# Steps 150 to 687 of a hand-written step list in a new order, in a fused clustered-attention and SiLU kernel

## The chip, the cores and the metric

The kernel runs on one core of a Trainium2 chip. The metric is device time in microseconds (us) of one execution; 302.02 us is the median of three runs of the kernel before (301.93 to 302.09).

## The reference

Attention over 4 batches and 8 heads, 768 tokens of 64 values each, in which a query attends only to keys whose nearest centroid (of 16 per head) is its own; its result, 3072 tokens of 512 values, goes through two matrix products with a SiLU between them.

```python
q_assign = np.argmax(np.einsum('bhsd,hcd->bhsc', q_n, c_n), axis=-1)
k_assign = np.argmax(np.einsum('bhsd,hcd->bhsc', k_n, c_n), axis=-1)
mask = q_assign[:, :, :, None] == k_assign[:, :, None, :]
scores = np.where(mask, scale * np.matmul(q, k.transpose(0, 1, 3, 2)), -1e9)
attn = softmax(scores)                      # over the keys
x = np.matmul(attn, v)                      # heads side by side: 3072 x 512
h = x @ w_in                                # 512 -> 2048
out = (h * sigmoid(h)) @ w_out              # 2048 -> 512
```

## The kernel before

**The order of the work is a list.** All the work after the first loads is issued by one list of 1559 words, `plan`, in the kernel's last function. Each word is a step: a name, a number, and behind a point either an engine (A is ACT, D is DVE, P is POOL) or the numbers of the PSUM banks that it opens. The function `step` turns a word into instructions. The kernel runs in a manual schedule, so the instructions of an engine, and the DMAs of a queue, are issued in the order of the list; semaphores keep only what depends on one another apart. An engine whose next instruction isn't ready waits with all that stands behind it. SP (the queue that issues most DMAs) and POOL (which issues some) are such queues too.

**Loading a head.** Job n is one head of one batch (32 in all; jobs 0 to 7 and two extra ones, `x`, carry batch 0). `r` loads its q and k in float32 (L92). `hi` scales them and rounds to float16 (L103 on ACT, L105 on POOL, L107 on DVE), `lo` takes the remainder (L112, DVE). `ht` transposes both by a DMA from SP into the tile `ab` (L121); in batch 0 `tr`, `xp` and `xq` do this on TensorE (PE) and `ev`, `xu`, `xw` copy it out of PSUM. `vl` loads v (L264, from SP or, with P, from POOL) and `v` rounds it (L270 on ACT, L272 on DVE or POOL).

**Assigning clusters.** `L`, `xL` and `l` multiply by the centroids (PE, L159), `ls`, `mx` and `ge` sum, find the maximum and compare (DVE, L168, L183, L192), `cm` transposes the marks (PE, L221), `ce` copies them out of PSUM (L232 on ACT, L234 on DVE) and sends them by a DMA from SP (L235) into rows of `ab`, where they act as the mask. From job 16 on `cs`, `cx` and `cv` do this by DMAs.

**Attention.** `qk` N (PE, L325, two products of 384 columns) writes scores into one of two PSUM buffers apart from the banks; `ex` N (ACT, L330) takes their exponential P. So `qk` N waits for `ex` N-2. There are 192 of them: 24 for each of 4 batches and 2 halves of the queries. `pa` to `py` and `pv` multiply P by v (PE, L342, 36 small products for two heads), `nm` normalizes (DVE, L352 and L354), and `pt` with `pe` (PE L363, then L372 on ACT or L374 on DVE), or `xd` (a DMA), transposes the result into `xt`.

**The SiLU part.** For each half of a batch there are 16 blocks: `e` (PE, L390, four products; `a` issues three of them ahead), `t` (ACT, tanh, L402), `g` (DVE, L405). The second matrix product is done for pairs of 128-token tiles with seven products instead of eight: `m` (PE, L477, eight matmuls each) on sums of tiles (`S`, DVE, L490) and on sums of weights (`wc`, DVE, L443), `z` and `o` write out. `w` loads the weights by DMAs from POOL (L526, L529), each behind a tiny copy (L522) that waits for the last `ex` listed ahead of it.

**Banks.** Four PSUM banks (0 to 3) are passed from step to step. A step that opens a bank waits for the step that read the earlier contents out: `e` for the `g` before it there, `pv` for a `nm`, `L` for a `ce`, `pt` for a `pe`, as the list says.

Of the kernel before, what the change touches and what calls it, by code (L numbers as in the profile page):

```python
# [29 lines left out]
def kernel(  # L30
# [573 lines left out]
    def step(op, n, eng, banks):  # L604
# [124 lines left out]
        w3 L7.1 w7 qk11 ex10 ex11 xL0.0 xM0 mx7 ge7 cm7 pb0 qk12 xm0 xg0 xh1.D ce7.A v2 xc0 pc0 xe0.D ex12 qk13 pa1.0  # L729
        qk14 pc1 nm0 pt0.3 w2 ex13 qk15 xl1 w5 v6.D pb1 hi8.D nm1 ex14 qk16 ex15 qk17 ex16 ex17 hi10.P w10 xq1.1 xp1.2  # L730
        xu1.D qk18 qk19 pa2.0 pb2 w6 w4 od0 v12.D xw1.D ex18 qk20 pt1.2 hi9.D pe1.D pc2 nm2 ex19 qk21 xL1.2 ex20 w8
        xM1 ex21 qk22 qk23 pt2.0 ex22 ex23 xm1 px3.1 qk24 pe0.D lo8 xg1 xc1 py3 qk25 ex24 qk26 pe2.D a1.0 xe1.A nm3
        pt3.1 pe3.D a0.2 ex25 ex26 qk27 ex27 e1 e4.1 e0 t4 g4 vl10 qk28 t0 g0 qk29 ex28 e6.3 t6 g6 ex29 vl11.P e3.1 t3
        w9 e2.2 t2 ht8 qk30 ex30 t1 qk31 g3 r12 lo9 w11 r13 e13.1 t13 g1 g13 qk32 pv4.3 g2 nm4 ex31 qk33 ex32 ex33
        vl14 e5.1 t5 qk34 ex34 lo10 g5 ht10 qk35 e11.3 qk36 ex35 qk37 pv5.0 nm5 ex36 t11 g11 pt4.2 qk38 wc0 ex37 e14.1
        qk39 ex38 ex39 hi11.D e8.0 ht9 lo11 pe4.A t14 t8 qk40 e12.2 ex40 ht11 g14 L8.3 qk41 qk42 t12 g12 ex41 ex42 g8
        mx8 ge8 e7.1 v11 qk43 e9.0 wc4 cm8 ce8.D v10 t7 g7 wc8 ex43 qk44 e10.1 qk45 t9 g9 wc1 hi13.A lo13 t10 S3 wc5
        wc2 e15.2 ex44 ex45 pt5.0 pe5.A wc9 qk46 L10.3 r14 ht13 r15 g10 hi12.A mx10 ex46 lo12 ht12 r17 qk47 ex47 ge10
        pv6.0 nm6 pv7.1 t15 g15 pt6.0 cm10 ce10.A l9.2 pe6.A wc6 nm7 pt7.1 pe7.A ls9 wc3 mx9 ge9 qk48 L11.2 ex48
        hi14.A e20.1 t20 l13.0 cm9.3 ce9.A mx11 ge11 wc12 cm11 ls13 qk49 qk50 ex49 g20 lo14 ht14 S1 e23.0 t23 ce11.A  # L740
        g23 e27.3 t27 g27 wc13 e18.1 t18 e16.2 wc7 hi15.A l12.0 ls12 e22.3 g18 ex50 t16 vl8 r18 wc10 g16 hi17.A lo15
        vl9 ht15 e21.0 t21 e25.1 t25 g21 g25 qk51 ex51 e30.2 t30 qk52 mx12 ge12 g30 r16 ex52 e29.0 t29 g29 e26.1 qk53
        qk54 t26 g26 t22 g22 lo17 ht17 e19.2 ex53 e24.1 cm12.0 L14.3 t19 g19 mx14 ge14 ex54 qk55 qk56 ce12.A t24 g24
        mx13 ge13 hi18.D r19 e31.2 ex55 ex56 l15.0 cm14 ce14.A ls15 e28.1 t28 g28 qk57 ex57 qk58 hi16.D e17.3 cm13.0
        m1.1 qk59 m7 lo16 wc14 S2 mx15 v8 ce13.A t31 ex58 t17 vl13 g17 ht16 od2 v9 pv8.0 nm8 qk60 g31 S13 ge15 ex59
        pv9.3 wc11 lo18 qk61 ex60 qk62 z0 m6 wc15 ex61 S4 qk63 cm15.0 vl15 ex62 ex63 m2.2 ht18 ce15.D z1 qk64 ex64 S11
        nm9 xd9 qk65 m5 v15 hi19.A ex65 v13 m11.0 m17 v14.D S12 qk66 z2 o3 lo19 ht19 ex66 l17.3 ls17 qk67 ex67 m3 qk68
        l16.3 r20 r23 xd8 mx17 ls16 o0 m4 qk69 ex68 z10 vl17 qk70 ex69 o1 ex70 pv10.2 od1 m16 ge17 cs17 z11 l18.3 qk71
        qk72 nm10 mx16 o2 xd10 r21 ex71 ex72 S23 ls18 m15 z12 o13 pv11.2 qk73 ex73 hi20.D ge16 nm11 m12.1 l19.3 m14
        S14 o12 ls19 lo20 o10 qk74 ex74 qk75 ex75 pt11.2 m13 pe11.A qk76 m21.3 mx18 mx19 r22 qk77 o11 e36.1 ex76 e34.0  # L750
        ex77 ht20 t36 z20 t34 qk78 ex78 m22.2 qk79 S21 S22 m26 cs16 ge18 ex79 hi21.D g34 o20 hi23.D lo21 pv12.2 vl18
        nm12 qk80 ht21 e35.0 qk81 z21 hi22.P ex80 t35 lo23 ex81 m25 z22 cx16 ht23 qk82 ex82 v18.D e37.2 m27 g36 o23
# [77 lines left out]
```

## Time and profile before

| what | value |
|---|---|
| time, median of 3 runs | 302.02 us |
| time of the profiled execution | 301.82 us |
| its span, first to last instruction | 300.0 us |
| granted TensorE clock | 0.999 |
| PE busy | 289.6 us, 97% |
| ACT busy | 235.3 us, 78% |
| DVE busy | 222.3 us, 74% |
| POOL busy | 67.1 us, 22% |
| DMA traffic | 44.13 MB, 147 GB/s over the span |

Around the span lie 1.82 us. Busy shares are means over a program whose stages differ, so they are read by stretches of time, given in us from the start of the span. A matmul of 384 columns is counted as busy for about 0.33 us, while in a row one follows the other after 0.16 us, so a PE that counts as busy can still be waiting a little. Steps 150 to 687 run from about 27 to 130 us.

### The profile page before, as it was taken

The numbers are of one execution on the slowest core, as the hardware profiler recorded it, in microseconds if no ns is written. First come the engines' busy times: TensorE is split into PE (matmuls) and PEld (weight loads), VectorE is DVE, ScalarE is ACT, GpSimd is POOL, SyncE is SP. The second block draws the span as 40 slices with busy tenths as digits, with TensorE's granted clock in tenths as the row PEclk, the third lists the DMA queues.
The fourth block names the chain that finished last, engine by engine and source line by source line (L and its number), as shares of the span: only waits on it lengthen the run. The fifth ranks groups of instructions, "written<-read, shape, count | busy, mean of one in ns | idle before, by whom it ended". The sixth has DMA issues, their size and how long they took to land.

```text
span 300.0 us, 8619 instructions
## 1 busy us (share of the span) xinstructions
PE 289.6 (97%) x3457; PEld 215.3 (72%) x3457; DVE 222.3 (74%) x488; ACT 235.3 (78%) x413; POOL 67.1 (22%) x121
## 2 busy tenths in 40 slices
PE   7899899889999999999999999999999999999995
PEld 3767666566688877767876787766866887777684
DVE  5898646899999597768758995788766734667673
ACT  5998899988988767898888975898759768974621
POOL 2656803000202004042664312111320000000000
PEclk9999999999999999999999999999999999999999
DMA  6999999999996899785569758479122102211103
GB/s 209 285 259 248 176 205 247 206 210 176 213 178 134 173 237 186 212 200 111 124 155 191 206 107 143 147 162 179 37 70 67 28 1 72 73 39 36 37 20 123
DMA packets 75688, 44.13 MB, mean 147 GB/s; under 512 B 54288, under 2 KB 71728, under 8 KB 75648
## 3 DMA queue, kind: packets, MB, share of 16 engines
q1 hardware_dynamic: 71136, 36.93, 53.8%
q0 software_dynamic: 4224, 6.36, 11.7%
q8 instruction: 27, 0.44, 0.6%
q10 hardware_dynamic: 288, 0.30, 0.3%
q14 instruction: 13, 0.11, 0.1%
HBM read 27.30 MB, written 6.29 MB: 112 GB/s over the span
## 4 chain that ended last, share of the span: by engine, by line
PE 79%; DMA 7%; DVE 5%; ACT 5%; issue 2%; POOL 1%; SPq 0%; ACTq 0%; POOLq 0%
PE ph L390 24%; PE xb L477 20%; PE pS L325 17%; PE pO L342 9%; DMA vn<-in_v_dram 5%; PE yb L477 3%; PE psN L159 3%; ACT P L330 2%; DMA raw<-in_q_dram 1%; DMA ab<-cd 1%; PE wb L477 1%; DVE hl L112 1%; DVE gt L405 1%; ACT hl L103 1%; ACT ab L144 1%
## 5 line engine op out<-in xcount | busy, mean ns | idle before, releaser
L330 ACT ACTIVATE P<-pS 128x768 f16<-128x768 f32 x192 | 151.2, 816 | 25.3 <-PE pS L325 24.7
L390 PE MATMUL ph<-xt,win_s 128*128 128x384 f16 x512 | 96.8, 326 | 1.6 <-DVE gt L405 1.0
L405 DVE SCALAR_TENSOR_TENSOR gt<-tn,ph 128x384 f16<-128x384 f32 x128 | 68.0, 550 | 27.8 <-ACT tn L402 26.9
L325 PE MATMUL pS<-ab 128*128 128x384 f16 x384 | 87.2, 326 | 1.1 <-DMA ab<-cd 0.6
L390 PEld LDWEIGHTS <-win_s 128*128 128x128 f16 x512 | 49.4, 98 | 33.4 <-issue 2.5
L402 ACT ACTIVATE tn<-ph 128x384 f32<-128x384 f32 x128 | 61.6, 500 | 12.5 <-PE ph L390 9.6
L325 PEld LDWEIGHTS <-ab 128*128 128x128 f16 x384 | 34.2, 97 | 16.4 <-issue 1.9
L342 PEld LDWEIGHTS <-P 128*128 128x128 f16 x1152 | 39.8, 97 | 4.1 <-ACT P L330 0.5
L477 PEld LDWEIGHTS <-gt 128*128 128x128 f16 x384 | 37.1, 98 | 7.2
L342 PE MATMUL pO<-vt,P 128*128 128x65 f16 x1152 | 41.2, 193 | 0.4 <-ACT P L330 0.4
L112 DVE SCALAR_TENSOR_TENSOR hl<-raw,hl 128x768 f16<-128x768 f32 (+3 forms) x35 | 31.9, 913 | 0.7 <-ACT hl L103 0.5
L477 PEld LDWEIGHTS <-s 128*128 128x128 f16 x288 | 27.9, 98 | 5.1
L272 POOL CAST vt<-vn 128x384 f16<-128x384 f32 x19 | 12.4, 661 | 55.1 <-DMA vn<-in_v_dram 55.1
L477 PE MATMUL xb<-wout_s,gt 128*128 128x256 f16 x192 | 24.6, 273 | 0.0
L499 ACT ACTIVATE ot<-xb 128x256 f32<-128x256 f32 x36 | 13.8, 384 | 11.5 <-PE xb L477 11.1
L477 PE MATMUL xb<-wc,s 128*128 128x256 f16 x176 | 22.8, 273 | 0.0
L159 PEld LDWEIGHTS <-ab 128*128 128x128 f16 x544 | 19.2, 97 | 4.3 <-issue 0.8
L199 POOL TENSOR_SCALAR od<-od 128x96 f16<-128x96 f16 x16 | 8.4, 525 | 55.0 <-DVE od L192 54.9
L159 PE MATMUL psN<-stk,ab 128*128 128x16 f16 (+1 forms) x544 | 20.0, 184 | 0.6 <-DVE xt L374 0.6
L105 POOL TENSOR_SCALAR hl<-raw 128x768 f16<-128x768 f32 (+1 forms) x8 | 16.3, 2034 | 12.9 <-ACT P L330 7.0
L354 DVE TENSOR_TENSOR xn<-pO,zr 128x384 f16<-128x384 f32 x32 | 17.8, 558 | 1.1
L508 DVE SCALAR_TENSOR_TENSOR ot<-xb,ot 128x256 f32<-128x256 f32 x20 | 8.5, 423 | 13.8 <-ACT ot L499 5.5
(90 smaller groups left out, 257.5 us busy)
## 6 DMA issues: line engine op xcount, KB each, us to landing
raw<-in_k_dram SPq DMA_DIRECT2D x31, 192.0 KB, 4.0
vn<-in_v_dram SPq DMA_DIRECT2D x25, 192.0 KB, 4.1
raw<-in_q_dram SPq DMA_DIRECT2D x24, 192.0 KB, 3.3
out_dram<-ot SPq DMA_DIRECT2D x18, 256.0 KB, 3.0
win_s<-in_moe_w_in_dram POOLq DMA_DIRECT2D x8, 256.0 KB, 7.1
wout_s<-in_moe_w_out_dram POOLq DMA_DIRECT2D x4, 512.0 KB, 9.6
out_dram<-ot SPq DMA_DIRECT2D x12, 128.0 KB, 1.7
vn<-in_v_dram POOLq DMA_DIRECT2D x7, 192.0 KB, 3.1
```

What stands on the lines that cost most here:

```text
L105: nc.gpsimd.tensor_scalar(out=o, in0=i, scalar1=QS, scalar2=None, op0=ALU.mult)
L112: nc.vector.scalar_tensor_tensor(out=hl[:, s, 1, :], in0=raws[job.name][:, s, :], scalar=QS, in1=hl[:, s, 0, :], op0=ALU.mult, op1=ALU.sub ...
L159: nc.tensor.matmul(L[:, n % 2, :, n // 2], ab[:, i, :], stk[:, job.groups[i // 3][0], x : x + w], start=(x == 0), stop=(x + w == 2 * HC),)
L325: nc.tensor.matmul(pS[:, e, 0:HALF], abs_[kj.name][:, kn, :], rhs, start=True, stop=True)
L330: nc.scalar.activation(out=P, in_=pst.pop(u)[:, :, 0:HALF], func=AF.Exp, bias=0.0, scale=ESC)
L342: nc.tensor.matmul(o[:, (2 * t + h) * VW : (2 * t + h + 1) * VW], Ps[i + h, c, j // 2][:, j % 2, ts(t, 128)], vtb[(i + h) % 13][:, j, 0:VW ...
L354: nc.vector.tensor_tensor(out=xn, in0=ov[:, :, 0:D], in1=zr.unsqueeze(2).to_broadcast([128, 2 * NM, D]), op=ALU.mult)
L390: nc.tensor.matmul(ph[:, 0:HALF], win_s[:, r, ts(fb, 128)], xts[b, c][:, r, :], start=(r == 0), stop=(r == NR - 1))
L402: nc.scalar.activation(out=tn, in_=phs[b, c, fb][:, 0:HALF], func=AF.Tanh, bias=0.0, scale=0.5)
L405: nc.vector.scalar_tensor_tensor(out=gt[:, fb, NM * c : NM * c + NM, :].rearrange("p t n -> p (t n)"), in0=tns.pop((b, c, fb)), scalar=1.0 ...
L477: nc.tensor.matmul(o, self.lhs(l, f), self.rhs(r, f), start=(f == 0 and opens), stop=(f == HB - 1), skip_group_check=True)
L499: nc.scalar.activation(out=o, in_=self.xb[:, 0:DH], func=AF.Copy, bias=0.0, scale=0.5)
```

## The change

The list is the only thing that differs. It has the same 1559 steps before and after; the first 150 and all from step 688 on are word for word the same. In between, steps stand in another order, and 75 have another engine or bank. Nothing is added or removed in the computation. One line of each, out of the 66 that differ:

```diff
-        xM1 ex21 qk22 qk23 pt2.0 ex22 ex23 xm1 px3.1 qk24 pe0.D lo8 xg1 xc1 py3 qk25 ex24 qk26 pe2.D a1.0 xe1.A nm3
+        pt0.3 xp1.0 xu1.D qk18 qk19 pa2.0 pc2 w10 vl11.P nm1 ex18 qk20 pb2 nm2 ex19 qk21 ex20 ex21 qk22 ex22 xL1.1
```

Steps that change engine: from ACT to DVE `xe1`, `pe4`, `pe5`, `pe7`, `hi17`, `ce14`, `pe11`; from DVE to ACT `pe1`, `ce8`, `hi16`, `hi20`, `v18`; from DVE to POOL `hi9`, `hi11`, `hi23`, `v17`; from POOL to ACT `v2`, `v13`, to DVE `v8`, `hi22`. The loads `vl10`, `vl15` and `vl16` go from SP to POOL. All others of the 75 change the bank alone. Of the places, these matter most below: `xL1` opens bank 1 (behind `pa1`) instead of bank 2 (behind `pt1`); `lo8` and `ht8` stand later; `a1`, `e1`, `t1`, `g1` go from about `ex27` to behind `ex42`; `wc4`, `wc5`, `wc1`, `wc2` stand earlier, and `w9`, `w11` stand behind `ex32` instead of `ex29` and `ex30`; `r14` stands ahead of `ce8`.

**ACT, from the exponential of step 12 on.** P is the exponential, `tn` the tanh, `cd` is `xe1`, `xt` is a `pe`, `vt` a rounded v. Before:

```order
L330 ACTIVATE P<-pS 128x768 x13
L232 ACTIVATE cd<-psN 96x256
L330 ACTIVATE P<-pS 128x768 x3
L402 ACTIVATE tn<-ph 128x384 x2
L330 ACTIVATE P<-pS 128x768
L402 ACTIVATE tn<-ph 128x384
L330 ACTIVATE P<-pS 128x768
L402 ACTIVATE tn<-ph 128x384 x2
```

The same place in the changed kernel:

```order
L330 ACTIVATE P<-pS 128x768
L270 ACTIVATE vt_72<-vn 128x6x64
L330 ACTIVATE P<-pS 128x768 x11
L372 ACTIVATE xt<-px 128x384
L330 ACTIVATE P<-pS 128x768 x4
L402 ACTIVATE tn<-ph 128x384
L330 ACTIVATE P<-pS 128x768
L402 ACTIVATE tn<-ph 128x384
L330 ACTIVATE P<-pS 128x768
```

`v2` and `pe1` have come to ACT, `xe1` has gone, and tanh and exponential take turns from the first tanh on.

**DVE, from the maximum of job 8 (`mx8`, the first row with `mxn`) on.** `om` is `ge8`, `wc` a sum of weights, `cd` is `ce8`, `zr` and `xn` are `nm5`, `s_97` is `S3`. Before:

```order
L183 TENSOR_REDUCE mxn<-psN 128x12
L192 TENSOR_TENSOR om_90<-psN,mxn 128x192
L443 TENSOR_TENSOR wc<-wout_s 128x512
L234 TENSOR_SCALAR cd<-psN,kadd 96x256
L405 SCALAR_TENSOR_TENSOR gt<-tn,ph 128x384
L443 TENSOR_TENSOR wc<-wout_s 128x512
L405 SCALAR_TENSOR_TENSOR gt<-tn,ph 128x384
```

The same place in the changed kernel, with the step ahead of `mx8` (`pe4`):

```order
L374 COPY xt<-px 128x384
L183 TENSOR_REDUCE mxn<-psN 128x12
L352 RECIPROCAL zr<-pO 128x6
L354 TENSOR_TENSOR xn<-pO,zr 128x384
L443 TENSOR_TENSOR wc<-wc,wout_s 128x512
L192 TENSOR_TENSOR om_90<-psN,mxn 128x192
L443 TENSOR_TENSOR wc<-wc,wout_s 128x512
L443 TENSOR_TENSOR wc<-wout_s,wc 128x512
L405 SCALAR_TENSOR_TENSOR gt<-tn,ph 128x384 x2
L443 TENSOR_TENSOR wc<-wout_s 128x512
```

`nm5`, three sums of weights that stood elsewhere and `g1` now stand behind `mx8`, and `ce8` has left DVE.

**SP, from the masks of `xe0` and `xe1` on.** Loads of `raw` are `r`, of `vn` are `vl`, the transposes are `ht8`, then `ht10`, `ht9`, `ht11`, and the last row is `ce8`. Before:

```order
L235 DMA ab<-cd 16x6x256 x2
L264 DMA vn<-in_v_dram 128x384
L121 DMA_TRANSPOSE ab<-hl 128x12x128
L92 DMA raw<-in_q_dram 128x384
L92 DMA raw<-in_k_dram 128x384
L92 DMA raw<-in_q_dram 128x384
L92 DMA raw<-in_k_dram 128x384
L264 DMA vn<-in_v_dram 128x384
L121 DMA_TRANSPOSE ab<-hl 128x12x128 x3
L235 DMA ab<-cd 16x6x256
```

The same place in the changed kernel:

```order
L235 DMA ab<-cd 16x6x256 x2
L121 DMA_TRANSPOSE ab<-hl 128x12x128
L92 DMA raw<-in_q_dram 128x384
L92 DMA raw<-in_k_dram 128x384
L264 DMA vn<-in_v_dram 128x384
L92 DMA raw<-in_q_dram 128x384
L92 DMA raw<-in_k_dram 128x384
L121 DMA_TRANSPOSE ab<-hl 128x12x128 x3
L92 DMA raw<-in_q_dram 128x384
L92 DMA raw<-in_k_dram 128x384
L235 DMA ab<-cd 16x6x256
```

One load of v has left the queue (`vl10`), the loads of job 14 now go ahead of the mask of `ce8`, and the transpose of job 8 is the next DMA behind `xe1`.

More of the change, by code (lines that the diff above doesn't have):

```diff
@@ L733 @@
[L733 to L752, printed above, removed]
@@ new lines @@
+        pt1.2 xM1 qk23 ex23 pe0.D xm1 px3.3 pt2.0 xg1 pe2.D pe1.A qk24 ex24 py3 nm3 qk25 a0.0 qk26 pt3.3 pe3.D xc1
+        xe1.D ex25 ex26 qk27 ex27 e0 hi9.P lo10 vl10.P qk28 lo9 t0 ex28 e3.3 t3 g3 qk29 ex29 g0 e4.1 qk30 t4 ex30 e2.2
+        t2 lo8 ht8 g2 qk31 pv4.3 nm4 ex31 qk32 ex32 g4 w9 e6.0 t6 e5.2 t5 g5 qk33 r13 w11 qk34 ex33 vl14 r12 e14.3
+        ex34 g6 t14 g14 e8.2 t8 g8 qk35 qk36 v12.D v11 hi11.P ex35 e12.0 t12 qk37 e11.2 ex36 qk38 pv5.3 ex37 qk39 g12
+        t11 g11 ex38 ex39 wc0 ht10 e13.2 pt4.0 lo11 wc4 ht9 t13 qk40 ht11 ex40 L8.1 qk41 g13 pe4.D ex41 v10 r14 mx8
```

105 lines of the change are left out of this document (60 added, 45 removed).

## The prediction, made before the changed kernel ran

> **What bounds the kernel now.** I read the busy time by stretches first, then who waits for whom, then single rows in order of time. The stretches are cut where the bound changes (columns: start:end, length, then busy us and instructions of PE, PE's weight loads, DVE, ACT and POOL, the granted clock, the DMA engines' share, GB/s).
>
> ```profile
> 27.00:42.00 15.00, 13.57 (x215) 9.84 (x216) 9.98 (x24) 12.45 (x18) 9.22 (x16) 1.00 1.04 182
> 42.00:57.00 15.00, 14.17 (x165) 9.25 (x164) 10.08 (x19) 14.45 (x27) 2.90 (x6) 1.00 1.21 234
> 58.44:77.97 19.53, 17.51 (x242) 12.25 (x241) 19.28 (x46) 17.44 (x34) 0.76 (x2) 1.00 1.06 199
> 78.00:130.00 52.00, 52.00 (x638) 40.56 (x636) 43.12 (x91) 42.28 (x75) 9.57 (x15) 1.00 0.88 192
> 130.00:300.00 170.00, 166.97 (x1831) 125.88 (x1828) 116.81 (x240) 125.04 (x226) 31.43 (x55) 1.00 0.43 99
> ```
>
> From 78 us on PE is full (52.00 of 52.00) up to the tail, and the change neither adds nor removes a product. So an order can win only ahead of 78 us, where PE has gaps: in 42 to 57 ACT is full (14.45 of 15.00), in 58.44 to 77.97 DVE is (19.28 of 19.53). What counts is how early PE has done the work that it has behind it when it becomes full; from there on the whole rest shifts by that much. PE's three longest waits in 27 to 80 us (waiter, releaser: us, times, longest):
>
> ```profile
> PE ph L390 <- DVE gt L405: 1.0, 2, 0.7
> PE psN L159 <- DVE xt L374: 0.6, 1, 0.6
> PE pS L325 <- DMA ab<-cd: 0.6, 1, 0.6
> ```
>
> The first two end with DVE. The third is a landing, `ce5`'s at `qk15`, and it was issued ahead of the part that changes.
>
> **The first term: ACT, up to `ex40`.**
>
> ```profile
> 30.26 2.25 ACT L330 ACTIVATE P<-pS 128x768 f16<-128x768 f32 x3 [0.80 <-PE pS L325]
> 36.76 2.25 ACT L330 ACTIVATE P<-pS 128x768 f16<-128x768 f32 x3 [0.89 <-PE pS L325]
> 54.78 0.48 ACT L372 ACTIVATE xt<-px 128x384 f16<-128x384 f16 x1
> 55.16 0.88 ACT L402 ACTIVATE tn<-ph 128x384 f32<-128x384 f32 x2
> 55.90 0.84 ACT L330 ACTIVATE P<-pS 128x768 f16<-128x768 f32 x1
> ...
> ACT P L330 <- PE pS L325: 2.8, 7, 0.9
> ```
>
> The single rows are ACT's in order of time (idle time before them in brackets); the last row sums ACT's waits for scores from 30 to 56.8 us. `ex40` ends at 55.90 + 0.84 = 56.74. Of the 2.8 us of waiting, 0.80 stands at `ex15`, behind the landing named above, and stays. The 0.89 stands at `ex22`, because PE was held at `xL1`, whose bank 2 had to be read out by `pe1` on DVE; now `xL1` takes bank 1, read out by a `nm1` that stands eleven steps ahead of it, so 0.89 goes. Left are 2.8 - 0.80 - 0.89 = 1.1 us at five places; bounds: all of it goes, or all comes back elsewhere. I take half, 0.55, since the new list lets each tanh alternate with an exponential from `ex27` on, but PE and ACT have nearly equal work there and will still meet. Work on ACT between `ex14` and `ex40`: `xe1`, `t1`, `pe4` leave, `pe1`, `t12` come, one small step less, 55.16 - 54.78 = 0.38. (`v2` comes to ACT too, ahead of `ex13`, in the shadow of the 0.80.) Together 0.89 + 0.55 + 0.38 = 1.82: `ex40` ends at **54.9**, with ends 54.4 and 56.36 (0.38 alone).
>
> **The second term: DVE, from `mx8` to `g25`.**
>
> ```profile
> 57.16 1.02 DVE L405 SCALAR_TENSOR_TENSOR gt<-tn,ph 128x384 f16<-128x384 f32 x2 [0.92 <-ACT tn L402]
> 58.09 0.35 DVE L183 TENSOR_REDUCE mxn<-psN 128x12 f32<-128x192 f32 x1
> ...
> 59.24 0.48 DVE L234 TENSOR_SCALAR cd<-psN,kadd 96x256 f16<-96x256 f32 x1
> ...
> 65.58 0.18 DVE L352 RECIPROCAL zr<-pO 128x6 f32<-128x6 f32 x1
> ...
> 66.27 0.54 DVE L405 SCALAR_TENSOR_TENSOR gt<-tn,ph 128x384 f16<-128x384 f32 x1
> ...
> 69.36 0.35 DVE L183 TENSOR_REDUCE mxn<-psN 128x12 f32<-128x192 f32 x1
> ...
> 70.03 0.42 DVE L443 TENSOR_TENSOR wc<-wout_s 128x512 f16<-128x512 f16 x1
> ...
> 72.76 1.01 DVE L405 SCALAR_TENSOR_TENSOR gt<-tn,ph 128x384 f16<-128x384 f32 x2
> 73.69 0.42 DVE L443 TENSOR_TENSOR wc<-wc,wout_s 128x512 f16<-128x512 f16 x1
> ...
> 76.95 1.01 DVE L405 SCALAR_TENSOR_TENSOR gt<-tn,ph 128x384 f16<-128x384 f32 x2
> ```
>
> Before, `mx8` ends at 58.09 + 0.35 = 58.44 and `g25` at 77.96; DVE idles 0.25 us between. In the new list nothing heavy can run on DVE ahead of `mx8`, since all stands behind it in the queue, and `mx8` needs `L8`, which PE does right after `qk40`. Ahead of it DVE has `g13` (0.55) and `pe4` (0.35), which start when `t13` on ACT ends, that is when `ex40` starts, 54.9 - 0.8 = 54.1; with 0.35 of its own `mx8` ends at 54.1 + 1.25 = **55.4**.
>
> Between `mx8` and `g25` DVE now has in addition: `nm5` (65.58 to 66.27: 0.69), `g1`, `g22`, `g30` (two from 72.76 to 73.69, so 0.465 each: 1.40), `mx12` and `ge12` (69.36 to 70.03: 0.67), `pe5` and `pe7` (0.35 less the 0.09 by which neighbours overlap: 0.52). It no longer has `ce8` (0.48 less 0.09: 0.39) and `wc4` (0.42 less 0.09: 0.33). Net 3.28 - 0.72 = 2.56. At the old density `g25` ends at 55.4 + 19.53 + 2.56 = **77.5**. Ends: no idle at all, 77.2; an idle 0.92 as at 57.16 once more, 78.4.
>
> **The third term: PE's work done by then.** `e19` opens bank 1, which `g25` reads out. It starts at 77.5, and ahead of it PE has in the new list, beside all that it had at 77.56 in the old one (where `e29` starts), six steps more: `qk53`, `qk54`, `e29`, `L14`, `cm12`, `qk55`.
>
> ```profile
> 77.56 1.46 PE L390 MATMUL ph<-xt,win_s 128*128 128x384 f16 x8
> 78.86 0.81 PE L325 MATMUL pS<-ab 128*128 128x384 f16 x4
> 79.51 1.53 PE L390 MATMUL ph<-xt,win_s 128*128 128x384 f16 x8
> 80.87 0.27 PE L221 MATMUL psC<-ident,om 128*96 128x128 f16 x2
> 80.98 0.76 PE L159 MATMUL psN<-stk,ab 128*128 128x16 f16 x24
> 81.59 0.65 PE L325 MATMUL pS<-ab 128*128 128x384 f16 x3
> ```
>
> From start to start: two `e` 1.30, two `qk` 0.65, `cm` 0.11, `L` 0.61. The six are 0.65 + 0.65 + 0.61 + 0.11 + 0.33 = 2.35, so the old kernel has as much done at 77.56 + 2.35 = 79.91. Gain: 79.91 - 77.5 = **2.4 us**.
>
> **Edits that I cost at nothing, and their cover.** `hi9` and `hi11` on POOL (POOL is busy 2.90 of 15.00 in 42 to 57) are done long before `lo9` and `lo11` ask for them; `lo11` lies ahead of the DVE stretch. Behind 78 us PE stays full: the moved sums, casts and stores lie beside products (DVE 43.12, ACT 42.28 of 52.00). The nearest row for what a late copy would cost there is the one landing wait, 0.6; I take 0 and keep 0.6.
>
> Two landings lie close. `wc8` on DVE needs the weights of `w11`, and everything on DVE is behind it; `qk48` needs the mask of `ce8`.
>
> ```profile
> 40.61 3.25 SPq L121 DMA_TRANSPOSE ab<-hl  x1
> ...
> 47.08 0.75 POOL L529 DMA_DIRECT2D wout_s<-in_moe_w_out_dram  x1 [0.55 <-issue]
> ...
> 59.96 1.09 SPq L235 DMA_DIRECT2D ab<-cd  x1
> ...
> 61.72 0.43 SPq L92 DMA_DIRECT2D raw<-in_k_dram  x1
> ...
> ab<-cd SPq DMA_DIRECT2D x1, 48.0 KB, 3.8
> ...
> wout_s<-in_moe_w_out_dram POOLq DMA_DIRECT2D x1, 512.0 KB, 10.8
> ...
> raw<-in_k_dram SPq DMA_DIRECT2D x1, 192.0 KB, 3.7
> ```
>
> The first four rows are issues (`ht8`, `w11`, `ce8`, the second half of `r14`), the last three the us to landing of three of them. `w11` was issued at 47.1 and took 10.8, so 57.9. Now it stands behind `ex32`, which ends some 1.8 us earlier than it did, and behind `w9`, so about 47.4 and 58.2; `wc8` is due behind `nm5`, three sums, `ge8` and two `g`, 55.4 + 0.69 + 0.99 + 0.27 + 0.93 = 58.3. Price 0 to 1 us, I take 0. `ce8` landed at 59.96 + 3.8 = 63.8; behind `r14`, whose second half landed at 61.72 + 3.7 = 65.4, it may be as late as 65.9. From `qk48` to `e19` PE has eight `qk`, ten `e`, two `L`, two `l`, three `cm`, two `pt`: 2.6 + 6.5 + 1.2 + 0.6 + 0.33 + 0.33 = 11.6 us (`l` at half an `L`, three transposes of a `pt` at half a `cm` each), so even 65.9 gives `e19` at 77.5, no later than DVE does. I take 0.
>
> **Sum.** From the profiled execution's own 301.82 (span 300.0 and 1.82 around it): 301.82 - 2.4 = 299.4. The median of the runs lies 0.2 above that execution, so **299.6 us**.
>
> **Rivals.**
>
> *Slower: the three transposes and `ce8` land late.* `ht8` went out at 40.6; now `lo8` stands on DVE behind `g0`, which needs the second tanh, so that I estimate 44.2, 3.6 later; the DMA engines are already oversubscribed there (share 1.21). If `ht10`, `ht9`, `ht11` and `ce8` slide by those 3.6 and `ce8` by another 1.6 behind `r14`, it lands at 69.0, and `e19` comes at 69.0 + 11.6 = 80.6, 0.7 later than the 79.91. That is 302.7. It decides from a landing of `ce8` at 68.3 on (79.91 - 11.6). Against it: `lo10` and `lo9` now stand ahead of `lo8`, so that the transposes behind `ht8` wait for nothing but the queue, and what DMA work lies ahead of them is the same.
>
> For this the Trainium skill ("DMA: Bandwidth & Descriptors", Issuing engines are not separate DMA queues) has a rule that speaks against the change: DMAs of all engines end up on the same 16 DMA engines and interleave, so that moving `vl10` from SP to POOL saves issue time alone. The share of 1.21 agrees with it, and by it the landings would stay where they are and the rest of the gain would hang on their slack; the sum above takes nothing for that move either.
>
> *Less: ACT's waits come back.* If only the 0.38 of work is saved, `ex40` ends at 56.36, `mx8` at 56.9, `e19` at 79.0: gain 0.9, 301.1. For it: PE and ACT are both nearly full in 42 to 57. Against it: 0.89 has a cause that the list removes.
>
> *More: both stretches run dense.* `ex40` at 54.4 and DVE without idle: `e19` at 54.9 + 19.28 + 2.56 = 76.7, gain 3.2, 298.8.
>
> *No effect:* a little of the second and third against each other, within the 0.2% (0.6 us) that a measurement can tell.
>
> **How the numbers follow.** The forecast, 298.9 to 300.4, has 0.50; less, 300.4 to 301.4, 0.14; more, 0.11; within 0.2%, 0.10; slower 0.15. So faster 0.75. The range is from 298.4 (the dense case with a little to spare) to 302.4, which takes in the bounds of the landings and leaves out the worse half of the slow case.
>
> **What would show it.** In the changed profile: ACT's 0.89 at `ex22` gone; `mx8` ending near 55.4; DVE full from there to about 77.5; `e19` then, and PE full behind it with the same end. It would be wrong if PE waits for `ab` behind a DMA at `L10`, `l9` or `qk48`, if DVE idles at `wc8`, or if PE has gaps behind 80 us.

## The result, and the profile after

The changed kernel takes **304.47 us** (median of 16 executions, 302.81 to 306.28); the kernel before, run beside it, 302.03 (16 executions, 301.23 to 303.66). The ratio is 1.0069, with a 95% interval of 1.0046 to 1.0091: slower by 0.7%, where 299.6 was forecast. Here and below, a median is that of all executions, while the ratio leaves out those over 1.5% above the fastest of their kernel, so the two need not agree to the last digit. The profiled execution took 306.28 us (span 304.4) and is the longest of the sixteen, so its account has more in it than the median.

First the busy time by stretches, cut as in the prediction, with the third stretch again from the end of `mx8` to the end of `g25` (changed kernel; columns as there):

```profile
27.00:42.00 15.00, 13.75 (x216) 10.16 (x216) 9.71 (x23) 13.57 (x20) 10.20 (x16) 1.00 1.12 203
42.00:57.00 15.00, 14.82 (x170) 9.75 (x169) 11.50 (x26) 14.60 (x26) 5.14 (x8) 1.00 0.92 181
55.61:80.82 25.21, 21.93 (x285) 14.95 (x283) 21.70 (x53) 20.39 (x37) 0.00 (x0) 0.93 1.07 198
80.82:130.00 49.18, 48.38 (x597) 38.11 (x595) 39.22 (x84) 39.65 (x68) 7.58 (x14) 1.00 0.84 192
```

Up to 57 us PE does more than before (14.82 against 14.17 of 15.00). The third stretch is the trouble: 25.21 us against 19.53, DVE busy 21.70 of it, PE's clock only 0.93. And behind it PE isn't full any more: 48.38 of 49.18. DVE in order of time around the first of these losses (changed kernel; idle time and its releaser in brackets):

```profile
55.26 0.35 DVE L183 TENSOR_REDUCE mxn<-psN 128x12 f32<-128x192 f32 x1
...
57.61 1.01 DVE L405 SCALAR_TENSOR_TENSOR gt<-tn,ph 128x384 f16<-128x384 f32 x2
61.42 0.43 DVE L443 TENSOR_TENSOR wc<-wout_s 128x512 f16<-128x512 f16 x1 [2.80 <-DMA wout_s<-in_moe_w_out_dram]
...
63.23 0.55 DVE L405 SCALAR_TENSOR_TENSOR gt<-tn,ph 128x384 f16<-128x384 f32 x1
```

`mx8` ends at 55.61. `wc8`, due at 58.6, stands 2.80 us for the weights of `w11`; `g9`, which is the last row, stands behind it. PE needs the bank that `g9` reads out (same kernel):

```profile
60.74 0.33 PE L363 MATMUL px<-ident,xn 128*128 128x128 f16 x3
63.83 0.80 PE L159 MATMUL psN<-stk,ab 128*128 128x16 f16 x24 [2.76 <-DVE gt L405]
64.47 1.44 PE L325 MATMUL pS<-ab 128*128 128x384 f16 x4
65.70 1.48 PE L390 MATMUL ph<-xt,win_s 128*128 128x384 f16 x4
...
81.16 1.46 PE L390 MATMUL ph<-xt,win_s 128*128 128x384 f16 x8
...
113.73 0.32 PE L390 MATMUL ph<-xt,win_s 128*128 128x384 f16 x1 [0.80 <-DVE xt L374]
...
166.27 0.52 PE L159 MATMUL psN<-stk,ab 128*128 128x32 f16 x12 [1.90 <-DMA ab<-hl]
```

`L10` waits 2.76 us. The four products of the third and fourth row take 1.44 and 1.48 us where four took 0.81 before: the clock was halved (last section). `e19` (81.16) starts 1.25 us later than the 79.91 at which the old kernel had as much done. Then PE waits 0.80 at `e35`, for the copy `pe11`, and 1.90 at `l24`, for a transpose in the part that the change left alone. 1.25 + 0.80 + 1.90 = 3.95 of the 4.46 us by which this execution is longer than the profiled one of before; the other half us is spread. The wait at `l24` isn't the change's own: in the kernels below it is sometimes there and sometimes not.

Why `w11` was late, from its issue and from its row in the view of the DMAs (KB, us to landing; changed kernel):

```profile
48.22 0.76 POOL L529 DMA_DIRECT2D wout_s<-in_moe_w_out_dram  x1
```

```profile
wout_s<-in_moe_w_out_dram POOLq DMA_DIRECT2D x1, 512.0 KB, 13.1
```

It went out at 48.22, 0.8 later than the forecast's 47.4, and flew 13.1 us where it had flown 10.8. The 47.4 is the place of `w9`, the other load of weights, which goes out at 47.33 (row below) with `w11` right behind it. In the kernel before, `w9` had a longer lead (its issue and its us to landing before, then its us to landing in the changed kernel):

```profile
45.25 0.75 POOL L529 DMA_DIRECT2D wout_s<-in_moe_w_out_dram  x1 [0.29 <-issue]
wout_s<-in_moe_w_out_dram POOLq DMA_DIRECT2D x1, 512.0 KB, 9.1
...
wout_s<-in_moe_w_out_dram POOLq DMA_DIRECT2D x1, 512.0 KB, 10.1
```

So `w9` landed at 54.4 before and at 57.4 after, 3.5 and 3.9 us ahead of `w11`. In the profiles of all kernels of this document `w11` lands 3.2 to 4.4 us behind `w9`, though it is issued only 0.9 to 1.8 behind it; its flight has part of that of `w9` in it. From the issue of `w9` to the landing of `w11`, below called the time of the pair, it took 12.6 us before and 14.0 after. Of the 3.45 us by which `w11` lands later (61.33 against 57.88), 2.1 are the later issue of `w9` and 1.4 the slower pair.

What the DMA engines did just ahead of that shows in their share (second column from the right), in the kernel before and then in the changed one:

```profile
42.00:44.00 2.00, 2.00 (x14) 1.22 (x13) 1.04 (x3) 2.00 (x6) 0.00 (x0) 1.00 1.21 207
44.00:46.00 2.00, 1.69 (x12) 0.88 (x10) 1.47 (x3) 2.00 (x5) 0.92 (x2) 1.00 1.15 290
46.00:48.00 2.00, 2.00 (x43) 1.68 (x42) 1.95 (x5) 1.98 (x5) 1.20 (x3) 1.00 1.24 221
```

```profile
42.00:44.00 2.00, 2.00 (x16) 1.23 (x15) 1.51 (x4) 2.00 (x5) 0.00 (x0) 1.00 0.79 224
44.00:46.00 2.00, 2.00 (x44) 1.61 (x43) 1.68 (x4) 2.00 (x4) 0.00 (x0) 1.00 0.16 45
46.00:48.00 2.00, 2.00 (x14) 1.19 (x13) 1.35 (x4) 1.92 (x5) 0.85 (x2) 1.00 1.15 203
```

From 44 to 46 us the DMA engines have next to nothing to do, 0.16 against 1.15. Both queues that feed them here stand: SP at `ht8`, which waits for `lo8`, and POOL at the tiny copy ahead of `w9`, which waits for `ex32` (SP from 41.2, when it had issued `xe1`, POOL for 9.27 us up to 46.51; SP's issues, then POOL's):

```profile
44.74 1.70 SPq L121 DMA_TRANSPOSE ab<-hl  x1
46.55 0.71 SPq L92 DMA_DIRECT2D raw<-in_q_dram  x1
...
49.21 13.86 SPq L121 DMA_TRANSPOSE ab<-hl  x3
```

```profile
46.51 0.18 POOL L522 COPY pace<-P 1x1 f16<-1x1 f16 x1 [9.27 <-ACT P L330]
47.33 0.77 POOL L529 DMA_DIRECT2D wout_s<-in_moe_w_out_dram  x1 [0.64 <-issue]
```

In 42 to 48 the share times the time is 2 x (1.21 + 1.15 + 1.24) = 7.2 us before and 2 x (0.79 + 0.16 + 1.15) = 4.2 after: 3.0 us of transfers that the old kernel had behind it are still to come. The share counts the time of packets, whatever their size; in bytes (the last column, GB/s, times the time) it is 1.44 MB before and 0.94 after. `ht10`, the transpose of job 10, also lands late, at 62.18 against 59.25. Whether this hole is the cause, or only a sight beside it, is a question for the experiments.

### The profile page after: what moved, and what is told of

It is laid out like the page before. It is cut to its first block, busy times and chain, and to the rows that moved or that the text cites. A ratio compares the mean times of both kernels' runs of the same rounds, so it can differ in the third digit from the quotient of the medians.

```text
span 304.4 us, 8635 instructions
## 1 busy us (share of the span) xinstructions
PE 290.7 (96%) x3457; PEld 215.9 (71%) x3457; DVE 220.3 (72%) x488; ACT 236.2 (78%) x413; POOL 67.7 (22%) x124
## 4 chain that ended last, share of the span: by engine, by line
PE 58%; DMA 4%; ACT 0%; issue 0%
PE ph L390 19%; PE xb L477 16%; PE pS L325 11%; PE pO L342 7%; DMA ab<-hl 4%; PE yb L477 3%; PE psN L159 1%; PE wb L477 1%; ACT ot L505 0%; PE px L363 0%
## 5 line engine op out<-in xcount | busy, mean ns | idle before, releaser
L390 PE MATMUL ph<-xt,win_s 128*128 128x384 f16 x512 | 98.0, 327 | 1.1 <-DVE xt L374 0.8
L112 DVE SCALAR_TENSOR_TENSOR hl<-raw,hl 128x768 f16<-128x768 f32 (+3 forms) x35 | 31.1, 894 | 0.5 <-ACT hl L103 0.3
L499 ACT ACTIVATE ot<-xb 128x256 f32<-128x256 f32 x36 | 13.9, 386 | 12.1 <-PE xb L477 11.8
L105 POOL TENSOR_SCALAR hl<-raw 128x768 f16<-128x768 f32 (+1 forms) x10 | 20.2, 2022 | 6.3 <-DMA raw<-in_q_dram 3.7
L272 POOL CAST vt<-vn 128x384 f16<-128x384 f32 x17 | 9.3, 553 | 44.9 <-DMA vn<-in_v_dram 44.2
```

Source lines behind the costliest of these rows:

```text
L105: nc.gpsimd.tensor_scalar(out=o, in0=i, scalar1=QS, scalar2=None, op0=ALU.mult)
L112: nc.vector.scalar_tensor_tensor(out=hl[:, s, 1, :], in0=raws[job.name][:, s, :], scalar=QS, in1=hl[:, s, 0, :], op0=ALU.mult, op1=ALU.sub ...
L390: nc.tensor.matmul(ph[:, 0:HALF], win_s[:, r, ts(fb, 128)], xts[b, c][:, r, :], start=(r == 0), stop=(r == NR - 1))
L499: nc.scalar.activation(out=o, in_=self.xb[:, 0:DH], func=AF.Copy, bias=0.0, scale=0.5)
```

## The experiments

Every kernel below computes the same as the others; only the list differs. Ratios are to the kernel before, run on the same chip, with 95% intervals. The theories of the first four: **A**, the one landing of `w11` at `wc8` costs the time, with the halved clock behind it; **B**, the losses are many, so that waits behind 100 us cost as well, and with `wc8` out of the way the next late landing holds PE. The first two kernels part the changed stretch in two, which is possible because both lists have done the same set of steps at step 428.

**s1_only: the first part alone.**

```diff
-words 150 to 428 as before
+words 150 to 428 as changed; all later words as before
```

> Steps 150 to 428 in the new order, everything behind them as before. Both orders have done the same steps at 428, so the change falls apart there. Theory A (the loss lies in one place: DVE stands at wc8 for the weights of w11, 2.80 us, and PE's clock is halved behind it): all of the loss is in this part, so about +2 us on the kernel before, 304 us, with DVE's wait at wc8 of 2 to 3 us. Rival B (late copies everywhere, also behind 100 us: the profile of the changed kernel shows waits of 0.97 at 113.7 and 2.06 at 166.3): at most +1 here, 302.5 to 303, and the rest of the loss in the other part.

Measured 303.89 against 301.82, ratio 1.0064 (1.0037 to 1.0091). The wait is there in the same size; DVE and PE of this kernel:

```profile
60.93 0.43 DVE L443 TENSOR_TENSOR wc<-wout_s 128x512 f16<-128x512 f16 x1 [2.84 <-DMA wout_s<-in_moe_w_out_dram]
```

```profile
63.34 0.75 PE L159 MATMUL psN<-stk,ab 128*128 128x16 f16 x24 [2.80 <-DVE gt L405]
```

So the first part alone shows nearly the whole loss, 2.07 us of 2.44, as A said.

**s23_only: the rest alone.**

```diff
-words 429 on as before
+words 429 on as changed; 150 to 428 as before
```

> Steps 150 to 428 as before, the rest in the new order. Theory A: within 0.6 us of the kernel before, 301.7 to 302.6. Rival B: 303 to 305, with the waits at 113.7 and 166.3 (shifted by less than 2 us) in the profile again.

Measured 302.93 against 301.82, ratio 1.0043 (1.0013 to 1.0072): 0.3 above A's range and just under B's. This part isn't free either: PE waits at `e35` for `pe11`, just as in the changed kernel. The losses of the two parts, 2.07 and 1.11, come to more than the 2.44 of the whole, so they don't simply add up.

```profile
112.24 0.32 PE L390 MATMUL ph<-xt,win_s 128*128 128x384 f16 x1 [0.80 <-DVE xt L374]
```

`pe11` stands in the new list on DVE behind `o12`, `S21` and `S22`, and `e35` needs its result. (The expectations give PE's waits 0.16 to 0.17 larger than the brackets do, 0.97 for this one; that is about the time at which one product follows another.)

In this kernel the weights have their old places, and still `w11` flew 12.6 us, where the profile of the kernel before has 10.8; the pair took 14.4:

```profile
wout_s<-in_moe_w_out_dram POOLq DMA_DIRECT2D x1, 512.0 KB, 12.6
```

So a flight of this load differs by 1.8 us from one profile to another without any help from the first part of the change.

**wc8_late: the waiting step moved, its wait left.**

```diff
-... e7.3 t7 g7 wc8 S3 qk43 ... ce11.A e23.0 wc9 t20 ...
+... e7.3 t7 g7 S3 qk43 ... ce11.A e23.0 wc8 wc9 t20 ...
```

> The changed kernel with the one step wc8 moved from behind g7 to just ahead of wc9, about 15 us later on DVE; nothing else. Theory A: DVE's 2.8 us and the halved clock go, PE then waits for the transpose of job 10 (landed at 62.2 while L10 would be due at 60.7) and for the mask of job 8 (landed 67.8): 1 to 2 us of the expected gain come, 300.5 to 302. Rival B: the next landing takes the place of w11's at once, and the time stays within 1 us of the changed kernel, 303.5 to 304.5.

Measured 305.65 against 301.82 (six executions), ratio 1.0103 (1.0060 to 1.0147): no better than the changed kernel, and above the ranges of both theories. DVE doesn't stand at 58.7 any more, and PE then waits at the same `L10` for the transpose of job 10:

```profile
63.11 0.77 PE L159 MATMUL psN<-stk,ab 128*128 128x16 f16 x24 [2.01 <-DMA ab<-hl]
```

`ht10` landed at 63.06, `w11` at 62.01. In this B is right: the landings are late together, and taking one waiter away uncovers the next. Why the time is over B's range as well isn't known; the clock halves in this profile, too (last section).

**w_early: the two weights go out earlier, nothing else.** `w9` and `w11` wait for `ex29` and `ex30` again, as before.

```diff
-... ex29 g0 e4.1 qk30 t4 ex30 e2.2 ... ex32 g4 w9 e6.0 ... r13 w11 qk34 ...
+... ex29 w9 g0 e4.1 qk30 t4 ex30 w11 e2.2 ... ex32 g4 e6.0 ... r13 qk34 ...
```

> The changed kernel with the loads of weights w9 and w11 behind ex29 and ex30, as before the change; only what the two tiny POOL copies wait for differs. The loads go out about 1.7 us earlier. If w11's flight stays at 13 us it lands at 59.7 and DVE still waits 1.1 us at wc8 instead of 2.8: 302.5 to 303. If the flight shrinks to the 10.8 us of before, since it then runs ahead of the loads that SP lets go at 46.5, it lands at 57.5 and the wait is gone: 300.5 to 302. Rival B: 303.5 to 304.5.

Measured 301.47 against 301.82, ratio 0.9994 (0.9971 to 1.0018): the loss is gone. `w11` goes out at 45.42, 2.8 us earlier, when little more than `w9` and `ht8` is in flight, and the same 512 KB take 8.8 us instead of 13.1:

```profile
wout_s<-in_moe_w_out_dram POOLq DMA_DIRECT2D x1, 512.0 KB, 8.8
```

The time of issue and the flight have both changed, and this run doesn't part them: 45.42 + 13.1 = 58.5 would also have been in time for `wc8`, which starts at 59.04 here. So it shows that the place of the weights makes the loss, and not that their flight does. The hole isn't enough to make it: this kernel has the same one (share 0.15 from 44 to 46 us). What is left in this kernel is a row of smaller waits of PE: 0.68 at 35.13 (the mask of `ce7`), 0.45 at `L8` and 0.65 at `l13` (transposes), 0.80 at `e35`. B's landings are now small, but still there.

**w_pe11: w_early, and `pe11` right behind `pt11`.**

```diff
-... nm11 pt11.1 o12 S21 qk77 ex76 S22 vl16.P qk78 v17 z20 o11 pe11.D e35.2 ...
+... nm11 pt11.1 pe11.D o12 S21 qk77 ex76 S22 vl16.P qk78 v17 z20 o11 e35.2 ...
```

> The changed kernel with w9 and w11 behind ex29 and ex30, and pe11 moved on DVE from behind S21 and S22 to right behind its pt11. Theory A2 (two places carry the loss: the late weights of w11, and 0.97 us at 111 to 115 us where PE's e35 waits for pe11): the 0.97 goes, so 0.9 to 1.0 under the kernel with the early weights alone, that is 300.5 us. Rival: e35 then waits for something else at the same place (its tanh or a bank) and the time stays at 301.5.

Measured 301.06 against 302.12, ratio 0.9952 (0.9925 to 0.9978), half a us over the expected 300.5. The wait at `e35` is gone from the profile (the profiled execution, 302.46, is the longest of twelve, with a wait at `l24`). The interval still overlaps a little with that of w_early, so the size of this gain is uncertain.

**s1_w_early: the first part with the weights early, the rest as before.**

```diff
-words 429 on as changed
+words 429 on as before; w9 and w11 as in w_early
```

> Steps 150 to 428 in the new order with w9 and w11 behind ex29 and ex30, everything behind step 428 as before the change. Theory A2: the part behind 428 costs its 0.97 at e35 and nothing else, so this is 0.9 to 1.0 under the kernel with the early weights, 300.4 to 300.6. If the new order behind 428 gains something on its own (the extra exponentials and products done early), this is no better than 301.5.

Measured 301.05 against 302.12, ratio 0.9955 (0.9932 to 0.9979), also half a us over what A2 expected. With its landing mended, the first part gains on its own what w_pe11 gains: the rest of the change adds nothing that these runs can tell.

Now why `w11` flies longer. **C**: the DMA engines ran half empty while SP stood at `ht8`, and all that came later is late by that much. **D**, later called 'crowd': `w11` runs among SP's transfers, which `ht8` held back and then let go all at once. A third, called 'order', was set against D in the later runs: it is late by its own place, behind `ex32` and `w9`, whatever SP does. Two kernels, in three runs, change SP and leave the weights where the change has them.

**ht8_early: SP doesn't stand at `ht8`.**

```diff
-... xc1 xe1.D ex25 ex26 ... e2.2 t2 lo8 ht8 g2 ...
+... xc1 xe1.D lo8 ht8 ex25 ex26 ... e2.2 t2 g2 ...
```

> The changed kernel with lo8 and ht8 moved from behind g0 to right behind xe1; w9 and w11 stay behind ex32. Theory C (the DMA engines ran half empty at 44 to 48 us, share 0.65, because SP stood at ht8, and all that came later was late by that much): ht8 goes out at about 41.6, w11 lands at 59 to 60 and the transpose of job 10 at about 59.5; DVE waits 1 to 1.5 us at wc8 instead of 2.8; 302 to 303. Theory D (what counts is that w11 was queued among the four loads and the transpose that SP let go in one go): with those out earlier w11 stands behind even more of them, lands at 61 or later, and the time stays at 304 to 305.

Measured 303.44 with a scatter from 300.61 to 307.56, ratio 1.0008 (0.9975 to 1.0041). The profile is of one of its longest executions, 307.31 us. Nothing is read from it, and the kernel ran once more.

**ht8_early_2: the same kernel again.**

> The same kernel as ht8_early a second time, for a profile of an ordinary execution. 'Crowd': the weights are issued while the loads and ht10 of SP are in flight, so w11 flies 12 us or more and wc8 and L10 wait 1.5 us or more, 302 to 304. 'Order' (w11 stands 0.8 us behind w9 and ht8 is no cause): the same wait as in the changed kernel, 2.8 us, 304.5.

Measured 304.02 against 302.05, ratio 1.0029 (0.9989 to 1.0070). This profile is of an ordinary execution (303.52):

```profile
61.27 0.42 DVE L443 TENSOR_TENSOR wc<-wout_s 128x512 f16<-128x512 f16 x1 [2.43 <-DMA wout_s<-in_moe_w_out_dram]
```

```profile
42.00:44.00 2.00, 2.00 (x15) 1.21 (x13) 2.00 (x4) 2.00 (x5) 0.00 (x0) 1.00 1.39 273
44.00:46.00 2.00, 2.00 (x43) 1.65 (x42) 1.10 (x4) 2.00 (x5) 0.00 (x0) 1.00 1.07 128
46.00:48.00 2.00, 2.00 (x15) 1.19 (x13) 1.35 (x3) 1.92 (x4) 0.65 (x2) 1.00 1.16 300
```

The hole is closed, 2 x (1.39 + 1.07 + 1.16) = 7.2 us of transfers as before (1.40 MB in bytes), and `w11` lands at 61.18 all the same. So C, which had it land at 59 to 60, is wrong for `w11`: in this profile it is late without the hole. D's landing, 61 or later, came out, but its picture is wrong: SP's five loads have all landed by 51.6, over nine us ahead of `w11`. The wait is 0.4 shorter than in the changed kernel; 'order' had said that it doesn't change. What the closed hole brought forward is `ht10`, which now lands at 55.85 instead of 62.18.

**loads_first: SP issues the three loads while it would stand at `ht8`.**

```diff
-... e2.2 t2 lo8 ht8 g2 ... qk33 r13 w11 qk34 ex33 vl14 r12 e14.3 ...
+... e2.2 t2 r13 vl14 r12 lo8 ht8 g2 ... qk33 w11 qk34 ex33 e14.3 ...
```

> The changed kernel with the loads r13, vl14 and r12 put ahead of lo8 and ht8, so that SP issues them while it would stand at ht8; the weights stay where the change has them (issued at 47.3 and 48.2). Theory 'crowd' (w11 flies 13.1 us because the loads and ht10 are let go together with it once ht8 is issued): with the loads gone by about 46, w11 lands by 59.5, wc8 waits under 1 us, PE's wait at L10 falls under 1, and the time is 301.5 to 302.7. Theory 'order' (w11 is late by its own place behind ex32, whatever SP does): w11 lands at 60.5 or later, wc8 waits 2 us or more, 304 to 305.

Measured 302.26 against 302.05, ratio 0.9993 (0.9960 to 1.0027). The time is what 'crowd' expected; the landing and the wait are those of 'order': `w11` (48.39) lands at 60.79, and DVE waits 2.09 for it. (The profiled execution, 303.13, is 0.9 above the median, so its wait may be longer than usual.)

```profile
60.88 0.42 DVE L443 TENSOR_TENSOR wc<-wout_s 128x512 f16<-128x512 f16 x1 [2.09 <-DMA wout_s<-in_moe_w_out_dram]
```

```profile
42.00:44.00 2.00, 2.00 (x14) 1.23 (x13) 1.51 (x4) 2.00 (x5) 0.00 (x0) 1.00 1.03 274
44.00:46.00 2.00, 2.00 (x43) 1.61 (x42) 1.68 (x5) 2.00 (x5) 0.00 (x0) 1.00 0.91 310
46.00:48.00 2.00, 2.00 (x15) 1.22 (x13) 1.35 (x3) 1.92 (x4) 0.69 (x2) 1.00 0.75 231
```

By the share, 2 x (1.03 + 0.91 + 0.75) = 5.4 us, 1.8 of the 3.0 are still missing; in bytes, 1.63 MB, nothing is. `w11` is late either way, so none of the three holds as I had put it. Two things can be read from the profiles themselves.

First, the time of the pair goes with what SP moves beside it. It is 9.7 to 9.8 us in w_early, w_pe11 and s1_w_early, where SP's queue takes 25 to 27% of the DMA engines' time meanwhile, and 12.6 to 14.7 us in the other profiles (without that of ht8_early), where it takes 57 to 70%. Second, given such a pair, the issue of `w9` decides: in the changed kernel, ht8_early_2 and loads_first it goes out at 47.3 to 47.5, and `w11` lands at 60.8 to 61.3, too late for a `wc8` that is due at 58.6 to 58.8.

All this fits a **backlog**: a transfer lands when what was let in ahead of it, and what shares the engines with it, is done. No run was made to test that picture against another. Nor does the slower pair of the changed kernel, 14.0 us against 12.6, need a cause in the change: in s23_only, with the old order up to step 428, the pair took 14.4.

**three: the three edits together.** The weights early as in w_early, `lo8` and `ht8` early as in ht8_early, `pe11` early as in w_pe11.

> The changed kernel with all three: w9 and w11 behind ex29 and ex30, pe11 right behind pt11, lo8 and ht8 right behind xe1. Theories A2 and C together: the waits for the transposes of jobs 8 (0.62 at 55 us) and 13 (0.82 at 68.6 us), which are left with early weights, shrink by half or more, 299.5 to 300.2, faster than the kernel before by 0.5% and more. Theory D: the early transposes push the weights back, and it is no faster than with early weights and pe11 alone.

Measured **299.79 us** (six executions, 299.46 to 300.5) against 302.12, ratio 0.9921 (0.9892 to 0.9949). It beats both kernels and lies 0.2 from the forecast, but with three edits that the forecast didn't have. Its DVE, its PE and its DMA shares:

```profile
55.44 0.35 DVE L183 TENSOR_REDUCE mxn<-psN 128x12 f32<-128x192 f32 x1
...
58.71 0.42 DVE L443 TENSOR_TENSOR wc<-wout_s 128x512 f16<-128x512 f16 x1
...
76.43 1.01 DVE L405 SCALAR_TENSOR_TENSOR gt<-tn,ph 128x384 f16<-128x384 f32 x2
```

```profile
61.11 0.75 PE L159 MATMUL psN<-stk,ab 128*128 128x16 f16 x24
...
77.78 1.46 PE L390 MATMUL ph<-xt,win_s 128*128 128x384 f16 x8
```

```profile
42.00:44.00 2.00, 2.00 (x14) 1.22 (x13) 2.00 (x4) 2.00 (x5) 0.18 (x1) 1.00 1.28 283
44.00:46.00 2.00, 2.00 (x44) 1.61 (x43) 1.10 (x4) 2.00 (x5) 1.39 (x3) 1.00 1.09 140
46.00:48.00 2.00, 2.00 (x14) 1.22 (x13) 1.35 (x3) 1.92 (x4) 2.00 (x3) 1.00 1.18 309
```

No idle time stands in brackets at `wc8` or `L10`; the transfers of 42 to 48 come to 7.1 us; `w11` lands at 57.33, 1.4 ahead of `wc8`. `w9` goes out at 44.61 here, and the pair takes 12.7 us: SP is as busy beside it as ever (62%), so it is the earlier issue that brings the weights in time. `g25` ends at 77.44 and `e19` starts at 77.78. On the same chip the median is 1.3 lower than that of w_pe11, which lacks only the early `ht8`, though the intervals overlap; the waits for the transposes at `L8` and `l13` are gone, as C had expected. One wait of PE over half a us is left in the middle of the program, 0.90 at 35.22, for the mask of `ce7`.

**three_ce7: that wait attacked.**

```diff
-... xc0 w2 xe0.D w8 pc0 nm0 xl1 ex12 qk13 ...
+... xc0 xe0.D pc0 nm0 xl1 ex12 w2 w8 qk13 ...
```

> Kernel three with w2 and w8 behind ex12, so that the mask of ce7 is issued ahead of them. If qk21's 1.06 us at 35 us is the landing of ce7 behind these weights, ce7 lands at 34.4 instead of 35.2, the wait falls to about 0.3 and the time to 299.1 (half a us less). If the us that PE saves there is taken back by ACT, which is nearly full from 42 to 57 us, it stays at 299.8.

Measured 300.81 against 302.05 (ten executions, 299.91 to 302.67), ratio 0.9952 (0.9920 to 0.9983), above both branches of the expectation. `ce7` did land at 34.4, as hoped, and PE's wait there fell from 0.90 to 0.15. But another landing came late in the profiled execution (301.45), the mask of `ce8`, 66.95 instead of 64.38:

```profile
67.00 0.50 PE L325 MATMUL pS<-ab 128*128 128x384 f16 x2 [2.19 <-DMA ab<-cd]
```

So what was won there was lost again in this execution, and against three nothing is gained. This is the wait at `qk48` of which the prediction's slower rival spoke, in a kernel where `ce8` lands 1.4 earlier than the rival's 68.3: how early a landing has to be depends on where PE is, and PE was earlier too.

**three_r14: `ce8` protected.** `r14` behind `ht13`, so that the mask goes out ahead of those loads.

```diff
-... ex41 v10 r14 mx8 ... ce8.A lo13 ht13 e9.0 ...
+... ex41 v10 mx8 ... ce8.A lo13 ht13 r14 e9.0 ...
```

> Kernel three with r14 behind ht13, so that the mask of ce8 goes out ahead of those two loads. In three ce8 landed at 64.4 and qk48 used it at 66.8, with 2.4 us to spare. If the place of r14 costs nothing, as the prediction had it, the time stays at 299.8 and ce8 lands about 1.2 us earlier; if ce8 is the landing that decides in some executions (in three_ce7 it landed at 66.95 and PE stood 2.36 us), the median falls to 299.5 and the spread shrinks; if r14 is now late itself, PE waits for a transpose behind 70 us and the time is 300.5 or more.

Measured 301.06 against 302.06, ratio 0.9960 (0.9940 to 0.9980). That is the third branch in its time, though the wait is another: `ce8` landed at 63.08, 1.3 earlier, but now ACT waits for `r14` itself, in `hi14`; the masks `ce9` and `ce11` stand behind that on ACT, and PE waits for the first of them to read a bank out:

```profile
68.42 0.84 ACT L103 ACTIVATE hl<-raw 128x768 f16<-128x768 f32 x1 [1.62 <-DMA raw<-in_k_dram]
...
69.87 0.46 ACT L232 ACTIVATE cd<-psC,kadd 96x256 f16<-96x256 f32 x1
```

```profile
70.38 2.14 PE L390 MATMUL ph<-xt,win_s 128*128 128x384 f16 x12 [0.99 <-ACT cd L232]
```

So the change's place of `r14`, ahead of `ce8`, looks well chosen, and nothing here speaks against the prediction's taking nothing for it; the intervals of three_r14 and three just overlap.

## Why the prediction was wrong, by its own steps

- **First term, ACT.** Forecast: `ex40` ends at 54.9. It ended at 55.25 before any of the losses. The 0.89 at `ex22` went, as the bank said. Of the five other waits, 1.1 us, I had left half; 0.20 stayed, but 0.68 came one exponential ahead of `ex22`, where `qk21` waits for the landing of `ce7`. So 0.88 stood for the forecast's 0.55. The main mechanism was right and the size off by 0.35; that it was off by no more is partly luck, as a wait that wasn't forecast stood in for those that went. (In the case "less", 56.36 - 0.8 + 1.25 is 56.8 and not 56.9, a slip on which nothing hangs.)
- **Second term, DVE.** Forecast: `mx8` at 55.4, then 22.09 us to the end of `g25`. `mx8` ended at 55.61. In three, where nothing waits at `wc8`, the stretch took 77.44 - 55.78 = 21.66, 0.4 less than forecast. This term was right, as far as a kernel with three more edits can show it.
- **Third term, PE.** Forecast: `e19` at 77.5 and 2.4 us gained. In three it starts at 77.78, 79.91 - 77.78 = 2.1 gained, and 302.12 - 299.79 = 2.3 in the medians. Right, with the same reserve.
- **The step that failed** stands under the edits costed at nothing: the landing of `w11` at `wc8`, "Price 0 to 1 us, I take 0". It measured 2.80 us on DVE and 2.76 on PE, and with the weights issued early (w_early) the wait and the loss are gone. The landing was put at 47.4 + 10.8 = 58.2 and came at 61.33, 3.1 later. Of these, 0.8 are the issue: 47.4 is the place of `w9`, and `w11` comes behind it. The other 2.3 are the flight: 10.8 was read where `w9` had a lead of 1.83 us in the same queue, and now it has 0.89, which accounts for 0.9 if the pair takes as long; but the pair took 1.4 longer as well, 14.0 for 12.6. These 1.4 are within what one order shows from profile to profile (12.6 before, 14.4 in s23_only), so a single flight was read as if it were fixed. The idle DMA engines from 44 to 46 us aren't shown to be the cause: w_early has the same hole and no loss, and with the hole closed (ht8_early_2) the pair still took 13.7. The bound of 1 us had no row behind it. Two of the signs named in advance showed the failure: DVE idles at `wc8`, and PE has gaps behind 80 us.
- **On top of the wait, the clock.** Of the 25.21 us from `mx8` to `g25`, 21.66 are the work (as in three) and 2.80 the wait; 0.75 remain, of which DVE spends 0.57 in one wait for PE's products `l9` at 67.57. Without the halved clock less remains: 0.10 in loads_first (23.85 - 21.66 - 2.09) and 0.11 in ht8_early_2 (24.20 - 21.66 - 2.43). So as far as three profiles show, most of the 0.75 goes with the halved clock. That a long wait can cost more than its length wasn't thought of.
- **Behind 78 us**, "PE stays full", bound 0.6: `e35` waited 0.80 for a copy, not for a landing. The rule by which I took 0, that copies lie beside products, overlooked that `pe11` stood behind three other DVE steps. The order of DVE's rows would have shown it.
- **The slower rival** had the right kind of mechanism, landings that slide after `ht8`, with the wrong decider. It asked for `ce8` at 68.3; `ce8` landed at 67.81, and `qk48`, which started at 68.60, didn't wait, since `L10` had lost more. Against the rival I held that "what DMA work lies ahead of them is the same". The work was the same, but by 48 us the changed kernel had done less of it (0.94 MB from 42 us on, against 1.44).
- **The shared DMA engines.** The prediction cites the Trainium skill ("DMA: Bandwidth & Descriptors", Issuing engines are not separate DMA queues) for the rule that transfers of all engines run on the same 16 DMA engines. These runs agree: issued at 45.4 to 45.5 us behind the same `w9`, `w11` flew 8.8 us in w_early, where SP's queue took 25% of the engines' time beside the pair, and 11.8 in three, where it took 62%. The error was in what I drew from the rule, that landings stay where they are as long as the amount of work is the same.

## What to carry to other kernels

A flight time read from a profile belongs to its place and to one execution: the transfer just ahead in the same queue and the traffic of the other queues are in it, and here it came out 1.8 us longer in another profile of the same order. When a change moves issues, reckon the landing from the first load of the group (here `w9`), and look at what the other queues will have in flight by then. Taking away the step that waits for a late landing is no cure if the landings are late together (wc8_late); issue the load with the least slack earlier. And where DVE sets the time, a copy that PE waits for belongs right behind the product that feeds it.

## What was not expected of the hardware

**The clock halves after waits of under 3 us.** In the profiled execution of the changed kernel (60 to 63.8, then on):

```profile
60.00:63.80 3.80, 1.07 (x9) 0.67 (x8) 2.38 (x5) 2.07 (x4) 0.00 (x0) 0.98 1.02 203
63.80:67.20 3.40, 3.37 (x39) 2.01 (x39) 3.17 (x8) 1.92 (x4) 0.00 (x0) 0.52 1.03 220
```

Behind 2.76 us of waiting PE ran 3.4 us at a granted clock of 0.52. The Trainium skill ("TensorE: Matmul & The Clock Gate", What's actually happening) has the clock fall to half after an idle window of about 3.4 us, in windows that run free of the program. The length of the slow stretch agrees; here the wait was shorter than the window that the rule names, and PE was busy for 0.8 of the 3.4 us ahead of the drop. In wc8_late it took even less: a wait of 2.01 us, with PE busy 1.21 of the 3.41 us up to 64.40, was followed by 3.41 us at 0.50. It doesn't happen in every execution: in the profiles of s1_only (wait 2.80), ht8_early_2 (2.40) and loads_first (2.06) the clock stayed at full.

Over 3.4 us, half a clock takes the mean of an execution to about 0.994, and this mean is on record for each. The changed kernel shows 0.994 in 10 of 16 executions, with a median of 304.92 us, and 0.999 or more in the other 6, with 302.94. In the five kernels in which the weights go out early and no wait of their profiles is over 2 us (w_early, w_pe11, s1_w_early, three, three_r14) no mean is that low in 54 executions. So the drop goes with the long wait, but not with it alone: means of 0.994 or less also stand in 5 of the 100 executions of the kernel before that ran beside the experiments and in 2 of 12 of s23_only, whose profiles have no such wait. How far the 2.0 us between the two groups are the clock's own, and not those of longer waits, stays open (in s1_only the groups don't differ in this way).

**The scatter of landings.** The wait at `l24` was 1.90 in the changed kernel's profile and absent in three's, though the list is the same in both from about 130 us on. (Counted from 0, as in the title, the last step that differs is 688.) The flight of `w11` in the old order, 10.8 and 12.6 us, is another case. What moves that landing stays open.
